# Tiny softmax sums, first value sums and three scales moved between engines in a two-level attention + two-FFN kernel

## The chip, the cores and the metric

The kernel runs on one core of one Trainium2 chip, in one launch. The metric is device time in microseconds (us), from three executions of each kernel. The engines are TensorE (PE; its weight loads are shown as PEld), VectorE (DVE), ScalarE (ACT), GpSimd (POOL) and SyncE (SP, which here issues nearly all DMAs). Each engine runs its own instructions in the order in which they were written down; they meet through semaphores.

## The reference

```python
# q, k, v: (4, 8, 576, 64) float32
q_d, k_d, v_d = means of four neighbouring rows               # 144 rows
out_up  = repeat(sm_attn(q_d, k_d, v_d), 4)                   # pooled attention
attn    = softmax(scale * q @ k.T where |i - j| < 4)          # local attention, 7 keys
a = a / (sum(a) + 1e-9)                                       # in both softmaxes
x = (out_up + attn @ v) as 2304 tokens x 512
h = x @ w_in;  g = where(h > 0, h, exp(min(h, 0)) - 1);  x = g @ w_out       # 512 -> 2048 -> 512
h = x @ w_in2; r = max(h, 0); g = s * r * r + b;         out = g @ w_out2
```

## The kernel before, in words

**Feed-forward part.** The 2304 tokens are nine blocks of 256. Each of the two FFNs (phases 0 and 1) works through 16 slices of 128 of the 2048 hidden columns for each block, so there are 144 pairs of block and slice in a phase. For each pair `ffn_h` issues 12 matmuls into a PSUM tile `h` and `ffn_x` 12 (phase 0) or 6 (phase 1, twice as wide) into `acc`. Every operand is split into a high and a low part of lower precision, hence three passes: `gh` and `gl` are the two parts of the activation, `w` holds both parts of a weight slice, which VectorE, ScalarE and GpSimd make from the loaded `raw` tile (L322 to L362).

**Attention part.** A unit is a pair of heads (`hp` 0 to 3) of one batch. Batch 0 runs first, before any FFN matmul can start: `tr` (transposes by TensorE, four-row sums by VectorE, L507), `gs` (pooled scores and their softmax, L542), `ls` and `softmax` (local scores, L625 and L647), `gpt_`/`lpt_` (transposes of the probabilities), `gpv`/`lpv` (times values, L604 and L705). The values summed in fours (`vd`) are needed by `gpv`. For batch 0 `vsum_pe` (L522) makes them with four matmuls by the identity per unit; for the other batches `vsum` (L533) makes them with two additions on GpSimd or VectorE. Batches 2 and 3 do the local attention without matmuls, in `direct` (L743). The second half of batch 0 and the batches 1 to 3 run between the FFN matmuls of phase 0.

**The sums.** Where ScalarE makes the exponentials, it also gives their sums (`sm`, an accumulator output); VectorE then adds 1e-9 and takes the reciprocal (L577, L685, L808).

**The order.** `Plan` (L55) takes every operation with an estimated cost and a due time (worked out from the constants at L29 to L32), plays them through and writes each engine's instructions down in the order it finds; it also picks between engines where an operation allows two. Where it sees TensorE idle, it puts filler matmuls on zeros (`wz`, L1131), as many as fill the planned gap. So every change of a cost or a constant reorders the whole program.

Of the kernel before, what the change touches and what calls it, by code (L numbers as in the profile page):

```python
# [6 lines left out]
F32 = mybir.dt.float32  # L7
# [21 lines left out]
T0, P0, LB, TR, R0, P1, P2 = 39.33, 5.045, 7, 29.37, 2.362, 2.546, 2.787  # L29
VO, N0, N1, WL, RL, A1, A2, A3, AE, XL = 13.82, -3.67, 51.83, 11.29, -7.8, 22.57, -17.87, 9.47, 64.11, 29.67  # L30
DE, DS, DT = 13.42, 98.08, 74.69
LASTP, NREST, VP = 2, 3, 2.0  # L32
# [22 lines left out]
class Plan:  # L55
# [172 lines left out]
def attn_moe_moe2(ctx, tc, q, k, v, w_in, w_out, w2_in, w2_out, s2, b2, mask, mask_d, out):  # L228
# [33 lines left out]
    ring = [p1.tile([QB, NQB, 2, D], F32, name=f"p{i}") for i in range(NLP)]  # L262
    nbufs["ring"] = NLP
# [110 lines left out]
    class Unit:  # L374
# [167 lines left out]
        def gs(self, heads, halves, due):  # L542
# [11 lines left out]
            nm, sm, s4, rs = (Buf(p2, t, [G, N2, 1]) for t in ("gnm", "gsm", "gs4", "grs"))  # L554
# [10 lines left out]
            op("dve", (0.1 + 0.15 * n) * len(heads) + 0.13 * (sc != 1.0), most, r=pss, w=[nmp], u=[nm], due=due)  # L565
# [14 lines left out]
            op("dve", 0.29, d2, r=[sm], w=[s4, rs], due=due)  # L580
# [4 lines left out]
        def gpt_(self, heads, halves, due):  # L585
# [14 lines left out]
            copy(pt, ps, 2 * n * m * G, r=[ps], w=[pt], due=due)  # L600
# [46 lines left out]
        def softmax(self, pss, half, due):  # L647
            F = 2 * NQB
            n = F * SW
            sc = Buf("ring", "p", None)  # L650
            sc.ring = ring
            part = lambda a: sc()[:, :, a, :SW]
            every = lambda: sc().rearrange("p m a w -> p (m a) w")[:, :, :SW]
            mx, sm, rs = (Buf(p2, t, [QB, F, 1]) for t in ("lmx", "lsm", "lrs"))

            by_act = self.b == 0 and self.hp % 2 < ACT_EXP
            for a, ps in enumerate(pss):
                h = slice(a, F, 2)
                if by_act:
# [28 lines left out]
            op("dve", 0.29 if by_act else 0.5 + n / 960, d2, r=[sc, sm], w=[sm, rs], due=due)  # L688
# [16 lines left out]
        def lpv(self, half, due):  # L705
# [10 lines left out]
            op("pe", 0.75, pe, r=[self.vwp[half], self.lpt[half]], w=[ps], u=self.both, due=due)  # L716
# [26 lines left out]
    def direct(b, t, due):  # L743
# [32 lines left out]
        sc = Buf(p2, "ds", [128, 4, 7])  # L776
# [8 lines left out]
        def scores(j):  # L785
# [5 lines left out]
                out=sc()[:, j:j + 2], in_=x(), axis=AX.X, op=ALU.add), r=[x], w=[sc], due=due)  # L791
# [11 lines left out]
        op("dve", 0.35, d1, r=[sc, c_sb2], w=[sc, mx], due=due)  # L803
        op("act", 0.2, lambda: nc.scalar.activation(out=sc(), in_=sc(), func=ACTF.Exp, scale=SCALE), r=[sc], w=[sc], due=due)

        def d2():
            nc.vector.tensor_reduce(out=sm()[:, :, 0], in_=sc(), axis=AX.X, op=ALU.add)
            nc.vector.tensor_scalar(out=sm(), in0=sm(), scalar1=1e-9, scalar2=None, op0=ALU.add)  # L808
            nc.vector.reciprocal(out=sm(), in_=sm())
            nc.vector.tensor_tensor(out=sc(), in0=sc(), in1=bc(sm), op=ALU.mult)  # L810

        op("dve", 0.75, d2, r=[sc], w=[sc, sm], due=due)

        def values(j):
# [3 lines left out]
               r=[vo, sc], w=[x], u=[rows_], due=due)  # L818
# [45 lines left out]
    def ffn_h(ph, j, f, n=N):  # L864
# [14 lines left out]
        us = 0.0075 + n / 2311  # L879
# [14 lines left out]
        if ph == 0:  # L894
            op("act", ta, lambda: nc.scalar.activation(out=e(), in_=ps(), func=ACTF.Relu, scale=-1.0),  # L895
# [19 lines left out]
    def ffn_x(ph, j, f, g):  # L915
# [5 lines left out]
        for a in range(2):  # L921
# [15 lines left out]
            op("pe", 0.70, pe, r=[w.out, gh, gl, acc], w=[acc], u=[w], due=due, ffn=True)  # L937
# [56 lines left out]
    def attention0():  # L994
# [12 lines left out]
        def Bs(u, d):  # L1007
            u.gs((0, 1), first, d), u.ls(0, d), u.vsum_pe(d + VP)
# [187 lines left out]
```

## Time and profile before

| | |
|---|---|
| median of 3 runs | 994.69 us (989.42 to 995.15) |
| the profiled execution | 995.36 us, of which the span is 993.6 us |
| busy share of the span | PE 97%, PEld 90%, DVE 64%, ACT 48%, POOL 41% |
| granted clock of TensorE, mean | 0.985 of full |
| first FFN matmul | 52.33 us after the span's start |

The busy time of TensorE counts fillers too, and counts a matmul at half clock in full. The 40 slices of the page show a clock of 0.8 and 0.5 in the first two slices and 0.9 or more in all others.

### The profile page before, as it was taken

To read this page: it belongs to the slowest core of one execution; us is meant where nothing else is said; L and a number is where in the kernel's file an instruction comes from. 1 tells how busy PE (TensorE), PEld (TensorE's weight loads), DVE (VectorE), ACT (ScalarE), POOL (GpSimd) and SP (SyncE) were. 2 spreads that over 40 slices of the span, in tenths; PEclk is the share of its full clock that TensorE was granted. 3 is DMA by queue.
4 is the path that set the end of the run, shared out by engine and by line. 5 is a ranking of instruction groups with operands and counts; after the bars stand their busy time and mean duration, and the time that the engine had idled before them with its cause. 6 is when DMAs were issued, how large, how long until landed. Compare 5 with 4: busy or idle time off the path is not lost.

```text
span 993.6 us, 21541 instructions
## 1 busy us (share of the span) xinstructions
PE 965.5 (97%) x8480; PEld 893.2 (90%) x8480; DVE 634.1 (64%) x1112; ACT 472.2 (48%) x1227; POOL 405.1 (41%) x358
## 2 busy tenths in 40 slices
PE   8999899998999999999999999999999999999998
PEld 6798888988989989999999999999999999999997
DVE  3478978888898989999637788433333343434332
ACT  4567566436444455444666675433333333333332
POOL 1245554688677787778465563100000000000000
PEclk8599999999999999999999999999999999999999
DMA  9556566435443353333335354001001010100000
GB/s 209 107 150 165 143 180 176 122 108 157 111 105 92 89 132 95 86 106 108 103 105 171 114 169 143 22 1 43 20 25 35 10 43 1 44 1 22 1 23 21
DMA packets 102469, 88.35 MB, mean 89 GB/s; under 512 B 48864, under 2 KB 91872, under 8 KB 102368
## 3 DMA queue, kind: packets, MB, share of 16 engines
q1 hardware_dynamic: 100576, 86.54, 31.4%
q8 instruction: 66, 1.08, 0.5%
q10 hardware_dynamic: 1792, 0.44, 0.2%
q14 instruction: 35, 0.29, 0.1%
HBM read 73.85 MB, written 13.11 MB: 88 GB/s over the span
## 4 chain that ended last, share of the span: by engine, by line
PE 48%; issue 3%; POOL 3%; DVE 3%; ACT 1%; SPq 0%; DMA 0%; POOLq 0%; DVEq 0%; ACTq 0%
PE h L875 24%; PE acc L934 20%; PE acc L931 4%; POOL gl L300 1%; POOL wu L300 1%; POOL w L300 1%; DVE raw L819 1%; DVE raw L351 1%; DVE r L899 0%; ACT raw L292 0%; DVE raw L353 0%; ACT r L895 0%; ACT w L292 0%; DVE wu L300 0%; ACT r L897 0%
## 5 line engine op out<-in xcount | busy, mean ns | idle before, releaser
L875 PE MATMUL h<-x,w 128*128 128x256 f32 x3264 | 430.6, 281 | 13.1 <-DVE r L899 10.8
L875 PEld LDWEIGHTS h<-x,w 128*128 128x128 f32 x3264 | 408.0, 188 | 30.7 <-DVE r L899 13.7
L931 PE MATMUL acc<-gh,w 128*128 128x256 f32 x1152 | 186.1, 283 | 0.0
L934 PE MATMUL acc<-w,gh 128*128 128x512 f32 x576 | 181.0, 395 | 0.0
L931 PEld LDWEIGHTS acc<-gh,w 128*128 128x128 f32 x1152 | 155.0, 188 | 2.5 <-issue 2.3
L905 DVE SCALAR_TENSOR_TENSOR r<-r,sb,h 128x256 f32<-128x256 f32 x144 | 68.8, 479 | 129.7 <-ACT r L904 128.6
L300 POOL TENSOR_TENSOR x<-xr,x 128x256 fp32r<-128x256 f32 (+2 forms) x43 | 43.1, 1021 | 264.0 <-DVE x L294 256.3
L300 POOL TENSOR_TENSOR gl<-r,gh 128x256 fp32r<-128x256 f32 x118 | 113.5, 967 | 59.3 <-ACT gh L292 52.5
L910 DVE SCALAR_TENSOR_TENSOR gl<-r,sb,gh 128x256 fp32r<-128x256 f32 x144 | 73.9, 513 | 99.2 <-ACT gh L908 99.2
L908 ACT ACTIVATE gh<-r,sb 128x256 fp32r<-128x256 f32 x144 | 73.4, 510 | 98.5 <-PE acc L934 89.4
L904 ACT ACTIVATE r<-h 128x256 f32<-128x256 f32 x144 | 55.1, 383 | 134.9 <-PE h L875 133.9
L931 PE MATMUL acc<-gl,w 128*128 128x256 f32 x576 | 114.4, 280 | 0.3 <-POOL gl L300 0.3
L934 PE MATMUL acc<-w,gl 128*128 128x512 f32 x288 | 114.0, 396 | 0.0
L934 PEld LDWEIGHTS acc<-w,gh 128*128 128x128 f32 x576 | 98.2, 188 | 14.1
L895 ACT ACTIVATE r<-h 128x256 f32<-128x256 f32 x144 | 54.7, 380 | 96.5 <-PE h L875 47.2
L300 POOL TENSOR_TENSOR w<-raw,w 128x512 fp32r<-128x512 f32 x47 | 64.2, 1379 | 78.7 <-ACT w L292 74.1
L899 DVE SCALAR_TENSOR_TENSOR r<-r,h 128x256 f32<-128x256 f32 x144 | 58.0, 412 | 49.4 <-ACT r L897 47.2
L931 PEld LDWEIGHTS acc<-gl,w 128*128 128x128 f32 x576 | 87.8, 188 | 0.9 <-POOL gl L300 0.7
L292 ACT ACTIVATE gh<-r 128x256 fp32r<-128x256 f32 x144 | 58.2, 413 | 52.6 <-DVE r L899 32.7
L934 PEld LDWEIGHTS acc<-w,gl 128*128 128x128 f32 x288 | 54.0, 188 | 13.0
L300 POOL TENSOR_TENSOR wu<-raw 128x896 f32<-128x896 f32 x29 | 61.5, 2135 | 9.3 <-DVE raw L819 9.3
L819 DVE TENSOR_REDUCE raw<-wu 128x128 f32<-128x896 f32 x36 | 63.5, 1783 | 2.1 <-POOL wu L300 2.0
(136 smaller groups left out, 1149.3 us busy)
## 6 DMA issues: line engine op xcount, KB each, us to landing
raw<-in_moe_w_in_dram SPq DMA_DIRECT2D x32, 512.0 KB
raw<-in_moe_w_out_dram SPq DMA_DIRECT2D x32, 512.0 KB
raw<-in_k_dram SPq DMA_DIRECT2D x17, 320.0 KB
raw<-in_v_dram SPq DMA_DIRECT2D x17, 320.0 KB
x2d<-ev SPq DMA_DIRECT2D x18, 256.0 KB
xr<-x2d SPq DMA_DIRECT2D x18, 256.0 KB
out_dram<-ev SPq DMA_DIRECT2D x16, 256.0 KB
vg<-in_v_dram SPq DMA_DIRECT2D x12, 288.0 KB
```

The lines of the kernel that those rows point to most:

```text
L292: a = (0.11 + n / 1200, lambda: nc.scalar.activation(out=out(), in_=src(), func=ACTF.Copy, scale=scale))
L300: f = lambda e: lambda: e.tensor_tensor(out=out(), in0=in0(), in1=in1(), op=alu)
L819: op("dve", 0.07 + 14 * D / 546, lambda: nc.vector.tensor_reduce(out=vo()[:, WD + j * D:WD + (j + 2) * D].rearrange("p (j d) -> p j d", j= ...
L875: nc.tensor.matmul(ps(), lhsT=w()[:, wpart, 0, c * 128:(c + 1) * 128], rhs=x()[:, xpart, c, :], start=first and i == 0, stop=last and i == ...
L895: op("act", ta, lambda: nc.scalar.activation(out=e(), in_=ps(), func=ACTF.Relu, scale=-1.0), r=[ps], w=[r1], u=[e], due=due)
L899: op("dve", td, lambda: nc.vector.scalar_tensor_tensor(out=e(), in0=e(), scalar=-1.0, in1=ps(), op0=ALU.add, op1=ALU.max), r=[r2, ps], w=[ ...
L904: op("act", ta, lambda: nc.scalar.activation(out=e(), in_=ps(), func=ACTF.Relu), r=[ps], w=[r1], u=[e], due=due)
L905: op("dve", td + 0.07, lambda: nc.vector.scalar_tensor_tensor(out=e(), in0=e(), scalar=sb2[:, 0:1], in1=ps(), op0=ALU.mult, op1=ALU.mult), ...
L908: op("act", ta + 0.1, lambda: nc.scalar.activation(out=gh(), in_=e(), func=ACTF.Identity, bias=sb2[:, 1:2]), r=[r2], w=[gh], u=[e], due=due)
L910: op("dve", td + 0.07, lambda: nc.vector.scalar_tensor_tensor(out=gl(), in0=e(), scalar=sb2[:, 1:2], in1=gh().bitcast(F32), op0=ALU.add, o ...
L931: nc.tensor.matmul(acc()[:, c * N:(c + 1) * N], lhsT=wo[:, cc * 128:(cc + 1) * 128], rhs=g(), start=(f == 0 and i == 0 and c == 0), stop=l ...
L934: nc.tensor.matmul(acc(), lhsT=g()[:, a * 128:(a + 1) * 128], rhs=wo, start=(f == 0 and i == 0), stop=last)
```

## The change

1. `vsum_pe` is gone; batch 0 uses `vsum` like the others, in place, with GpSimd or VectorE.
2. The tiles into which ScalarE writes sums are kept for the whole program, with a second column beside each sum that is filled with 1e-9 once; VectorE reduces the two columns (`TENSOR_REDUCE`) where it added a constant before (`TENSOR_SCALAR`). In the softmaxes that VectorE sums itself, 1e-9 stands in the column behind the scores and is summed with them.
3. The factor 4 of the pooled softmax moves into the eviction of the transposed probabilities (0.25 in `gpt_`); the factor on the row maxima moves from VectorE to ScalarE.
4. Costs of the planner, its due-time constants and the order that follows from them are changed.

```diff
-T0, P0, LB, TR, R0, P1, P2 = 39.33, 5.045, 7, 29.37, 2.362, 2.546, 2.787
+T0, P0, LB, TR, R0, P1, P2 = 39.86, 4.909, 5, 35.22, 2.265, 2.616, 2.881
...
-    GROUP = 9.0
+    GROUP = 12.52
...
+             "gsm": [p1.tile([G, 2, 2], F32, name=f"gsm{i}") for i in range(2)],
+             "lsm": [p1.tile([QB, 2 * NQB, 2], F32, name=f"lsm{i}") for i in range(2)],
+             "ds": [p1.tile([128, 4, 8], F32, name=f"ds{i}") for i in range(2)]}
...
-        def vsum_pe(self, due):
...
-                for r in range(4):
-                    nc.tensor.matmul(ps(), lhsT=ident[:G, :G], rhs=self.vg()[:, :, r * D:(r + 1) * D],
-                                     start=(r == 0), stop=(r == 3))
...
-               r=[self.vg], w=[self.vg, self.vd], due=due, lock=True)
+               r=[self.vg], w=[self.vg, self.vd], u=self.both + self.tdv if self.b == 0 else (), due=due, lock=True)
...
-                if sc != 1.0:
-                    nc.vector.tensor_scalar(out=nm(), in0=nm(), scalar1=sc, scalar2=None, op0=ALU.mult)
...
+                    if j == 0 and sc != 1.0:
+                        nc.scalar.activation(out=nm(), in_=nm(), func=ACTF.Copy, scale=sc)
...
-                nc.vector.tensor_scalar(out=s4(), in0=sm(), scalar1=1e-9, scalar2=4.0, op0=ALU.add, op1=ALU.mult)
+                nc.vector.tensor_reduce(out=s4()[:, :, 0], in_=sm()[:, :N2], axis=AX.X, op=ALU.add)
...
-            copy(pt, ps, 2 * n * m * G, r=[ps], w=[pt], due=due)
+            copy(pt, ps, 2 * n * m * G, scale=0.25, r=[ps], w=[pt], due=due)
...
-                if not by_act:
-                    nc.vector.tensor_reduce(out=sm()[:, :, 0], in_=every(), axis=AX.X, op=ALU.add)
-                nc.vector.tensor_scalar(out=rs(), in0=sm(), scalar1=1e-9, scalar2=None, op0=ALU.add)
+                x = sm() if by_act else sc().rearrange("p m a w -> p (m a) w")[:, :, :SW + 1]
+                nc.vector.tensor_reduce(out=rs()[:, :, 0], in_=x, axis=AX.X, op=ALU.add)
...
-            nc.vector.tensor_reduce(out=sm()[:, :, 0], in_=sc(), axis=AX.X, op=ALU.add)
-            nc.vector.tensor_scalar(out=sm(), in0=sm(), scalar1=1e-9, scalar2=None, op0=ALU.add)
+            nc.vector.tensor_reduce(out=sm()[:, :, 0], in_=ds(), axis=AX.X, op=ALU.add)
...
-            u.gs((0, 1), first, d), u.ls(0, d), u.vsum_pe(d + VP)
+            u.gs((0, 1), first, d), u.ls(0, d), u.vsum(d + VP)
...
+        for t in rings["gsm"] + rings["lsm"] + rings["ds"]:
+            nc.gpsimd.memset(t, 1e-9)
+        for t in rings["p"]:
+            nc.gpsimd.memset(t[:, :, :, SW:SW + 1], 1e-9)
```

How the order moves, at three places. First TensorE in the attention of batch 0, before the first FFN matmul. Here `w_287` and `w_302` are the loaded values of a unit, `w_150` its loaded queries and keys, `w_360` its transposed ones, `s` the pooled and `p` the local probabilities. The kernel before:

```order
L512 MATMUL at<-ident,w_150 128x96 x3
L527 MATMUL acc<-w_287,ident 72x256 x4
L595 MATMUL h<-ident,s 72x72 x4
L612 MATMUL h<-pt,w_209 64x72 x4
L550 MATMUL acc<-w_360 72x144 x2
L713 MATMUL h<-pt,w_224 64x32 x18
```

The same stretch in the changed kernel:

```order
L523 MATMUL at<-ident,w_293 128x96 x3
L598 MATMUL h<-ident,s 72x72 x4
L615 MATMUL h<-pt,w_224 64x72 x4
```

The sum by the identity (L527) no longer stands between the transposes and the products; there are four such rows of four matmuls in the kernel before and none in the changed one.

Second GpSimd at the start of the program, the kernel before (`lrs` and `grs` are the reciprocals of the sums):

```order
L1142 MEMSET p_87 96x384
masks.py:197 MEMSET ident 128x128
masks.py:199 ISA
masks.py:199 AFFINE_SELECT ident<-ident 128x128
L300 TENSOR_TENSOR p_85<-p_85,lrs 96x6x38
L300 TENSOR_TENSOR s<-s,grs 72x288 x2
```

And the changed kernel:

```order
L1149 MEMSET p_87 96x6
masks.py:197 MEMSET ident 128x128
masks.py:199 ISA
masks.py:199 AFFINE_SELECT ident<-ident 128x128
L536 TENSOR_TENSOR w_160<-w_160 72x4x128
L537 TENSOR_TENSOR w_224<-w_160 72x256
L311 TENSOR_TENSOR p_85<-p_85,lrs 96x6x38
L311 TENSOR_TENSOR s<-s,grs 72x288
L536 TENSOR_TENSOR w_242<-w_242 72x4x128
L537 TENSOR_TENSOR w_306<-w_242 72x256
```

The two additions of each unit (L536, L537) stand ahead of the normalizations in GpSimd's queue; nine small memsets more stand ahead of the identity.

Third VectorE in the softmaxes of the first unit, the kernel before:

```order
L685 TENSOR_SCALAR lrs<-lsm 96x6
L686 RECIPROCAL lrs<-lrs 96x6
L577 TENSOR_SCALAR gs_345<-gsm 72x2
L578 RECIPROCAL grs<-gs_345 72x2
```

And the changed kernel:

```order
L686 TENSOR_REDUCE lrs<-lsm_90 96x6
L687 RECIPROCAL lrs<-lrs 96x6
L580 TENSOR_REDUCE gs_362<-gsm_88 72x2
L581 RECIPROCAL grs<-gs_362 72x2
```

The constant is now read from the tile beside the sum, by a reduction.

Over the whole program VectorE has 949 rows where it had 1012, GpSimd 282 where it had 262, ScalarE 1004 where it had 968. The fillers, counted in TensorE's order, stand at other places, though there are 599 where there were 588: 187 before the first FFN matmul (153 before the change); 231 (376) from there to the 721st FFN matmul; 110 (27) from the 721st to the 865th, a stretch that holds the start of the third token block (its first matmul is the 769th); 71 (32) after that. SP issues the values of a unit (288 KB and 216 KB) ahead of the next unit's keys and queries, where it issued the keys and queries of all four units first.

## Rows read from the trace of the kernel before

**Rows 1.** The page: busy time, share and instructions of TensorE.
```profile
PE 965.5 (97%) x8480; PEld 893.2 (90%) x8480; DVE 634.1 (64%) x1112; ACT 472.2 (48%) x1227; POOL 405.1 (41%) x358
```

**Rows 2.** Busy time by stretch: length, PE, PEld, DVE, ACT, POOL, clock, DMA share, GB/s.
```profile
16.00:46.00 30.00, 30.00 (x298) 21.54 (x297) 12.39 (x38) 15.69 (x67) 7.43 (x11) 0.50 0.69 153
75.00:100.00 25.00, 23.60 (x418) 21.53 (x417) 20.46 (x41) 18.07 (x64) 14.27 (x14) 1.00 0.60 161
100.00:225.00 125.00, 117.25 (x1515) 108.84 (x1513) 106.32 (x202) 69.69 (x178) 76.99 (x68) 1.00 0.54 145
225.00:475.00 250.00, 241.17 (x2101) 232.81 (x2097) 228.82 (x358) 123.83 (x364) 192.38 (x155) 1.00 0.41 107
600.00:990.00 390.00, 389.57 (x2492) 350.79 (x2490) 154.66 (x311) 141.38 (x308) 25.43 (x26) 1.00 0.07 24
```

**Rows 3.** Timeline of TensorE: start, length, line, operands, count, idle before.
```profile
5.38 0.69 PE L512 MATMUL at<-ident,w 96*128 96x96 f32 x6
...
14.92 3.48 PE L527 MATMUL acc<-w,ident 72*72 72x256 f32 x8
18.33 0.76 PE L550 MATMUL acc<-w 64*72 64x144 f32 x4
...
39.47 3.62 PE L527 MATMUL acc<-w,ident 72*72 72x256 f32 x8
42.89 3.78 PE L1135 MATMUL at<-wz 128*128 128x128 bf16 x40
...
52.33 0.95 PE L875 MATMUL h<-x,w 128*128 128x256 f32 x6
...
62.68 1.74 PE L1135 MATMUL at<-wz 128*128 128x128 bf16 x28
```

**Rows 4.** Durations (ns, min/median/max) of the two additions on GpSimd, later batches.
```profile
L536 POOL TENSOR_TENSOR vg<-vg x10: 1270/1373/2273, 78.7 to 376.3; 72x512 f32<-72x512 f32 x10
L537 POOL TENSOR_TENSOR vd<-vg x10: 722/736/1568, 80.1 to 377.8; 72x256 f32<-72x256 f32 x10
```

**Rows 5.** Groups of VectorE by form: busy us, mean ns; idle before.
```profile
L577 DVE TENSOR_SCALAR gs<-gsm 72x2 f32<-72x2 f32 x32 | 18.2, 569 | 1.5 <-ACT s L571 1.2
L685 DVE TENSOR_SCALAR lrs<-lsm 96x6 f32<-96x6 f32 x16 | 5.7, 354 | 1.9 <-ACT p L667 1.6
L563 DVE TENSOR_SCALAR gnm<-gnm 72x2 f32<-72x2 f32 x16 | 5.0, 313 | 0.5
L808 DVE TENSOR_SCALAR dsm<-dsm 128x4 f32<-128x4 f32 x18 | 4.6, 255 | 0.6
L807 DVE TENSOR_REDUCE dsm<-ds 128x4 f32<-128x28 f32 x18 | 3.2, 176 | 0.3 <-ACT ds L804 0.3
```

**Rows 6.** Timeline of GpSimd and VectorE around 404 us.
```profile
403.53 1.69 POOL L300 TENSOR_TENSOR wu<-raw,ds 128x896 f32<-128x896 f32 x1 [2.61 <-issue]
403.68 1.56 DVE L577 TENSOR_SCALAR gs<-gsm 72x2 f32<-72x2 f32 x1
```

**Rows 7.** Waits of TensorE over the span: total us, times, longest.
```profile
PE h L875 <- DVE r L899: 10.8, 15, 2.3
```

**Rows 8.** Timeline of GpSimd at the start: memsets and the identity.
```profile
0.34 0.11 POOL L1179 MEMSET const-uint8-127<- 128x1 uint8 x1
0.73 1.12 POOL L1142 MEMSET p<- 96x384 f32 x3 [0.29 <-POOLq L1179]
...
2.07 0.29 POOL masks.py:199 TENSOR_SCALAR_AFFINE_SELECT ident<-ident 128x128 f32<-128x128 f32 x1
```

**Rows 9.** Timeline of ScalarE: its smallest activation.
```profile
4.18 0.20 ACT L1017 ACTIVATE warm<-wz 128x1 bf16<-128x1 bf16 x1
```

**Rows 10.** Timeline of TensorE at the third token block.
```profile
227.10 3.30 PE L875 MATMUL h<-x,w 128*128 128x256 f32 x24
```

**Rows 11.** Two stretches of 4 us, columns as in Rows 2.
```profile
12.00:16.00 4.00, 2.98 (x19) 2.07 (x20) 2.12 (x7) 2.45 (x8) 1.19 (x2) 0.88 0.98 195
96.00:100.00 4.00, 2.98 (x54) 2.63 (x50) 1.12 (x4) 2.34 (x6) 2.56 (x2) 1.00 0.25 100
```

More of the change, by code (lines that the diff above doesn't have):

```diff
@@ L61 @@
     SLACK = 0.0
-    GROUP = 9.0
-    SWITCH = 0.024
-    HOLD = 0.089
-    WAIT = 1.512
+    GROUP = 12.52
+    SWITCH = 0
+    HOLD = 0.057
+    WAIT = 1.597
     STORE = 2.5
@@ L261, in attn_moe_moe2, with kept @@
     msk = p1.tile([QB, 2, NQB, SW], BF16, name="msk")
-    ring = [p1.tile([QB, NQB, 2, D], F32, name=f"p{i}") for i in range(NLP)]
-    nbufs["ring"] = NLP
+    rings = {"p": [p1.tile([QB, NQB, 2, D], F32, name=f"p{i}") for i in range(NLP)],
+             "gsm": [p1.tile([G, 2, 2], F32, name=f"gsm{i}") for i in range(2)],
+             "lsm": [p1.tile([QB, 2 * NQB, 2], F32, name=f"lsm{i}") for i in range(2)],
+             "ds": [p1.tile([128, 4, 8], F32, name=f"ds{i}") for i in range(2)]}
+    for tag, tiles in rings.items():
+        nbufs[tag] = len(tiles)
+    def kept(tag):
+        b = Buf(tag, tag, None)
+        b.ring = rings[tag]
+        return b
     mskd = p1.tile([128, 2, 28], BF16, name="mskd")
@@ L553, in gs @@
             op("pe", 0.25 * N2 / len(heads) + 0.1, pe, r=[self.d], w=pss, u=self.tdv, due=due)
-            nm, sm, s4, rs = (Buf(p2, t, [G, N2, 1]) for t in ("gnm", "gsm", "gs4", "grs"))
+            nm, s4, rs = (Buf(p2, t, [G, N2, 1]) for t in ("gnm", "gs4", "grs"))
+            sm = kept("gsm")
             e = Buf(p2, "s", [G, N2, 2 * G])
@@ L561, in most @@
                     nc.vector.tensor_reduce(out=nm()[:, j * n:(j + 1) * n, 0], in_=ps(), axis=AX.X, op=ALU.max, negate=True)
[L562 to L565 removed]
+            op("dve", (0.1 + 0.15 * n) * len(heads), most, r=pss, w=[nmp], u=[nm], due=due)
             for j, ps in enumerate(pss):
                 def ac(j=j, ps=ps):
+                    if j == 0 and sc != 1.0:
+                        nc.scalar.activation(out=nm(), in_=nm(), func=ACTF.Copy, scale=sc)
                     for i in range(n):
@@ L649, in softmax @@
             n = F * SW
-            sc = Buf("ring", "p", None)
-            sc.ring = ring
+            sc = kept("p")
             part = lambda a: sc()[:, :, a, :SW]
             every = lambda: sc().rearrange("p m a w -> p (m a) w")[:, :, :SW]
-            mx, sm, rs = (Buf(p2, t, [QB, F, 1]) for t in ("lmx", "lsm", "lrs"))
+            mx, rs = (Buf(p2, t, [QB, F, 1]) for t in ("lmx", "lrs"))
             by_act = self.b == 0 and self.hp % 2 < ACT_EXP
+            sm = kept("lsm") if by_act else None
             for a, ps in enumerate(pss):
@@ L714, in pe @@
                                          rhs=pt[o:o + SW, i * SB:(i + 1) * SB], start=True, stop=True)
-            op("pe", 0.75, pe, r=[self.vwp[half], self.lpt[half]], w=[ps], u=self.both, due=due)
+            op("pe", 1.24, pe, r=[self.vwp[half], self.lpt[half]], w=[ps], u=self.both, due=due)
             x = Buf(p2, "xs", [128, G, 4])
@@ L775, in direct @@
         load(vo, 327680, lambda: window(v, vo), due - 6, u=[rows_])
-        sc = Buf(p2, "ds", [128, 4, 7])
+        ds = kept("ds")
+        sc = Buf(None, "sc", None)
+        sc.view = lambda: ds()[:, :, :7]
         mx, sm = (Buf(p2, x, [128, 4, 1]) for x in ("dmx", "dsm"))
@@ L877, in mm @@
             return pe
-        us = 0.0075 + n / 2311
+        us = 0.0085 + n / 2311
         w_hi, w_lo = w.part
@@ L935, in pe @@
                                          start=(f == 0 and i == 0), stop=last)
-            op("pe", 0.70, pe, r=[w.out, gh, gl, acc], w=[acc], u=[w], due=due, ffn=True)
+            op("pe", 0.712, pe, r=[w.out, gh, gl, acc], w=[acc], u=[w], due=due, ffn=True)
             if f == FC - 1:
@@ L1140, in attn_moe_moe2 @@
         nc.vector.memset(wz, 0.0)
-        for t in ring:
+        for t in rings["p"]:
             nc.gpsimd.memset(t, 0.0)
+        for t in rings["gsm"] + rings["lsm"] + rings["ds"]:
+            nc.gpsimd.memset(t, 1e-9)
+        for t in rings["p"]:
+            nc.gpsimd.memset(t[:, :, :, SW:SW + 1], 1e-9)
         make_identity(nc, ident)
```

37 lines of the change are left out of this document (18 added, 19 removed).

## The prediction

> **What bounds the kernel now.** I read the page first, then the busy time by stretch, then TensorE's timeline at the start, then the groups of VectorE, and last the waits. TensorE is busy in 965.5 of 993.6 us [rows 1], so the time is the length of its instruction stream plus 28.1 us of idle. From 600 us on there is nothing to gain: 389.57 of 390 us are busy, and these are FFN matmuls alone [rows 2]; the change leaves them as they are. What can move lies before 600 us, in two places. One is the start. From 16 to 46 us TensorE is busy without a gap, at a granted clock of 0.50, that is 1.2 instead of 2.4 GHz [rows 2], and the first FFN matmul stands at 52.33 us [rows 3]. In this stretch TensorE itself is the bound: VectorE works 12.39 of 30 us, ScalarE 15.69, GpSimd 7.43. The other place is the stretch from 75 to 475 us. There TensorE's idle is 1.40 + 7.75 + 8.83 = 18.0 us, and VectorE is the fullest of the engines that feed it: 228.82 of 250 us in the last part [rows 2].
>
> **The change part by part.** The sum is made against the profiled execution, 995.36 us, which lies 0.1% above the median of 994.69.
>
> *The value sums leave TensorE.* One of them takes from 14.92 to 18.33 us, 3.41 us from its first matmul to the next instruction, and the last one from 39.47 to 42.89, 3.42 us [rows 3]. There are four: 4 x 3.42 = 13.7 us of a stream that has no gap here. I take the whole, **-13.7 us**. At the high clock the same columns would take about half, so an end of -6.8 us stands for a start that isn't throttled.
>
> *Fillers.* The changed order has 34 more before the first FFN matmul (187 against 153). At the low clock 40 fillers take 3.78 us [rows 3], 94.5 ns each: **+3.2 us**. After it there are 23 fewer (412 against 435), and at the high clock 28 take 1.74 us [rows 3], 62 ns each: **-1.4 us**. Their places matter more than their number: 145 fewer up to the 721st FFN matmul (-9.0 us), 83 more around the start of the third block (+5.1), 39 more behind it (+2.4).
>
> *The sums arrive on GpSimd.* The two additions have medians of 1.37 and 0.74 us [rows 4], 2.1 us a unit, 8.4 us for four. GpSimd is idle for three quarters of the start, so most of it is covered. But GpSimd runs in order, and the normalizations `p` and `s` stand behind the additions, which in turn wait for their values to land; TensorE's next transposes wait for `p` and `s`. If one of the four sums shows, that is 2.1 us; if none, 0; if all, 8.4. I take **+2 us**, since GpSimd has only 7.43 us of other work in 30 us.
>
> *The loads change places.* 504 KB of values now stand ahead of the keys and queries of the third unit. The DMA engines move 195 GB/s there [rows 11], so these come about 2.6 us later. At worst the third unit's transposes wait all of it, at best they would have waited for something else until then; between 0 and 2.6 us I take **+1 us**, the lower half, since the queue in front of them is the same length otherwise.
>
> *The memsets at the start.* Nine more stand ahead of the identity, which is ready at 2.36 us [rows 8]; TensorE first uses it at 5.38 us [rows 3]. The nearest small memset takes 0.11 us, the wide ones 0.4 [rows 8], so the identity moves to 3.4 us, or to 6.0 at worst. Zero, or 0.6 us if the cover is gone.
>
> *VectorE's small operations.* An operation on two elements a lane, `gs`, takes 569 ns on average and 18.2 us in all [rows 5], because it is held up: one began at 403.68 and lasted 1.56 us, until 5.24, while an addition on GpSimd ran from 403.53 to 405.22 [rows 6]. A reduction of 28 elements to 4 takes 176 ns, evenly [rows 5]. With 176 ns for each reduction, `gs` gives back 32 x (569 - 176) = 12.6 us, `gnm` 5.0 (it goes to ScalarE), `dsm` 4.6 (it falls away), `lrs` 5.7 - 8 x 0.176 = 4.3 (eight fall away, eight become reductions): 26.5 us of VectorE's time. The Trainium skill speaks against this edit (VectorE: DVE Perf Modes, Rules for kernel authors): a reduction runs at the lowest rate and is the slowest operation of VectorE, so restructure. By that rule nothing of the 12.6 us would come back; the rows above decide for the reduction at these sizes. On the path I count the 26.5 us as **0**: TensorE's idle in this stretch is small, and a held operation may only hand its hold-up to the next one. At most it is TensorE's own waiting for `r` of VectorE, 10.8 us [rows 7]; at least nothing, since less work on VectorE costs nobody time. The 16 scalings on ScalarE take 0.20 us each [rows 9], 3.2 us in all, while four evictions of the value sums go; ScalarE is half idle, and in the chain of one softmax the scaling only changes its engine. Zero. GpSimd takes over some splits from VectorE; it works 192.38 of 250 us from 225 to 475 us [rows 2], so its spare time covers them. The 0.25 rides on an eviction that is there anyway. Zero each.
>
> Sum: -13.7 + 3.2 - 1.4 + 2 + 1 = -8.9 us, and 995.36 - 8.9 = **986.4 us**.
>
> **The rivals.**
>
> *VectorE was the bound in the middle.* For it: VectorE is 92% busy from 225 to 475 us, and TensorE's largest wait in the list is the one for its `r`, 10.8 us [rows 2, 7]. Against it: TensorE itself is 96% busy there. If that goes as well, the time is 986.4 - 10.8 = 975.6 us. The Trainium skill has a rule that weakens this rival (SBUF: State Buffer, SBUF: two separate sides): VectorE and GpSimd share one port pair, which one instruction holds to its end. The trace agrees, with 1.56 us at 403.68 [rows 6], and an operation with two inputs that follows would be held in the same way.
>
> *The third block doesn't come earlier, and the kernel is slower.* The first FFN matmul of the third block stands at 227.10 us [rows 10]. Its input is what the attention of batch 1 wrote to memory, a chain through all engines in which VectorE is 106.32 of 125 us busy [rows 2]. If that chain isn't shortened, everything won before is waited away there, and the changed order itself stalls at this place with 110 fillers where there were 27. What is left is the 39 later fillers, +2.4 us: 997.8 us. It decides as soon as the third block starts no earlier than 227 us. Against it: the chain starts from the same attention of batch 0, which ends earlier, and VectorE has less to do. Partly true, it would end between 987 and 995.
>
> *The clock falls a second time.* Before the fall at about 15.5 us TensorE was busy 2.98 of 4 us, and the low clock then lasted until about 46 us [rows 2, 11]. The changed order has 145 fewer fillers between the first FFN matmul and the third block. If TensorE really waits there, 30 us at half clock cost 15 us: 986.4 + 15 = 1001.4 us. Against it: from 96 to 100 us it was also busy only 2.98 of 4 us and the clock stayed at 1.00 [rows 11].
>
> *GpSimd doesn't keep up at the start.* All four sums show, 6.4 us more: 992.8 us. It is in the forecast's range.
>
> **How the numbers follow.** Chances: the forecast 0.50, VectorE as the bound 0.25, the third block partly or wholly unmoved 0.19, the clock 0.06. The forecast's own range is 980 to 993: down to 980.1 where nothing new is waited for (3.0 us) and a third of the 10.8 us comes back (3.6), up to 993 where all four sums show. From 975 to 997 the range takes in VectorE's case and the third block's but for its far end. A difference of 1%, 10 us, is about what a measurement of this kernel can tell from no change; it lies at 984.7 us, inside the forecast's range. So faster by over 1% has VectorE's 0.25 and a third of the forecast, 0.41 together; slower by over 1% needs the clock and more, 0.05; within 1% the rest, 0.54.
>
> **What would show it.** Right: no matmuls by the identity into `acc`, the first FFN matmul at 43 to 48 us, the reductions `gs` at 0.15 to 0.2 us each, the third block at 215 to 222 us, and 390 us that are the same from there on. Wrong at the sums: TensorE idle behind `p` or `s` of GpSimd before 45 us. Wrong at VectorE: the same idle of TensorE although VectorE's busy time falls by 25 us, or idle that falls below 10 us. Wrong at the third block: its first matmul at 227 us. The clock: a second stretch at 0.5.

## The result and the profile after

The changed kernel takes 983.21 us (median of 20 runs, 980.57 to 987.69), the kernel before 994.4 us on the same chips (20 runs, 984.55 to 998.75). The ratio is 0.9911, 95% interval [0.9887, 0.9934]: 8.9 us less, which is the forecast's sum to the tenth. (The medians differ by 11.2: the runs of the kernel before lie in three groups, about 985, 989 and 994 us and up, and the ratio weighs them all.) That the sum came out so is luck: the experiments show errors of both signs that cancelled. The profiled span is 981.8 us (993.6 before).

The page of the changed kernel, busy time of each engine, to be held against [rows 1]:

```profile
PE 961.0 (98%) x8459; PEld 897.8 (91%) x8459; DVE 614.9 (63%) x1055; ACT 475.3 (48%) x1242; POOL 409.6 (42%) x387
```

TensorE has 961.0 of 981.8 us busy, so 20.8 us idle instead of 28.1. That is only 4.5 us less busy time, although 13.7 us of value sums are gone: something else on TensorE has become longer.

Busy time by stretch, columns as in [rows 2]:

```profile
12.00:16.00 4.00, 3.47 (x68) 2.86 (x68) 2.80 (x11) 2.70 (x12) 2.98 (x4) 1.00 1.20 214
16.00:46.00 30.00, 29.54 (x508) 26.72 (x506) 20.11 (x44) 19.76 (x81) 17.98 (x20) 0.94 0.88 216
75.00:100.00 25.00, 24.16 (x300) 22.22 (x297) 23.06 (x36) 17.93 (x47) 16.06 (x16) 1.00 0.54 163
100.00:225.00 125.00, 118.86 (x1454) 111.08 (x1455) 107.06 (x194) 71.81 (x194) 75.90 (x75) 0.99 0.57 157
225.00:475.00 250.00, 246.57 (x2112) 240.64 (x2111) 206.63 (x314) 120.37 (x344) 182.33 (x150) 1.00 0.37 100
```

The largest difference is in the second row: from 16 to 46 us the clock is 0.94 instead of 0.50, and TensorE gets through 508 instructions instead of 298. In the whole profile the clock falls three times before the last microseconds, at about 31, 62 and 212 us, for 3.4 us each. From 75 to 475 us TensorE is idle for 0.84 + 6.14 + 3.43 = 10.4 us instead of 18.0.

TensorE's timeline, columns as in [rows 3]: the load that the values now stand ahead of, the first FFN matmul, and the start of the third block (cf. [rows 10]):

```profile
12.47 0.79 PE L523 MATMUL at<-ident,w 96*128 96x96 f32 x6 [0.76 <-DMA w<-in_k_dram]
...
32.69 3.14 PE L1138 MATMUL acc<-wz 128*128 128x128 bf16 x36
35.64 0.95 PE L878 MATMUL h<-x,w 128*128 128x256 f32 x6
...
202.62 1.90 PE L1138 MATMUL acc<-wz 128*128 128x128 bf16 x31
204.33 1.22 PE L878 MATMUL h<-x,w 128*128 128x256 f32 x8
```

The first FFN matmul stands 16.7 us earlier (52.33 before), the third block 22.8 us (227.10 before). The kernel ends only 11.8 us earlier. The rest is lost again.

GpSimd at the start, columns as in [rows 8]: the identity, the first unit's two additions, and the normalization behind them:

```profile
2.44 0.29 POOL masks.py:199 TENSOR_SCALAR_AFFINE_SELECT ident<-ident 128x128 f32<-128x128 f32 x1
9.41 1.27 POOL L536 TENSOR_TENSOR w<-w 72x512 f32<-72x512 f32 x1 [6.68 <-DMA w<-in_v_dram]
10.76 0.73 POOL L537 TENSOR_TENSOR w<-w 72x256 f32<-72x256 f32 x1
11.85 0.56 POOL L311 TENSOR_TENSOR p<-p,lrs 96x228 f32<-96x228 f32 x1 [0.36 <-DVE gs L580]
```

The additions wait for the values to land, but the normalization behind them then waits for VectorE (0.36 us), not for them.

VectorE's groups, columns as in [rows 5]: the three reductions, and two operations with two inputs that follow or stand near them:

```profile
L311 DVE TENSOR_TENSOR w<-raw,w 128x512 fp32r<-128x512 f32 x17 | 21.9, 1288 | 1.1 <-ACT w L303 1.1
L814 DVE TENSOR_TENSOR ds<-ds,dsm 128x28 f32<-128x28 f32 x18 | 7.6, 421 | 0.6
L580 DVE TENSOR_REDUCE gs<-gsm 72x2 f32<-72x4 f32 x32 | 4.6, 144 | 2.4 <-ACT s L572 2.3
L810 DVE TENSOR_REDUCE dsm<-ds 128x4 f32<-128x32 f32 x18 | 3.2, 180 | 2.0 <-ACT ds L807 2.0
L686 DVE TENSOR_REDUCE lrs<-lsm 96x6 f32<-96x12 f32 x8 | 1.2, 154 | 0.9 <-ACT p L669 0.9
```

The reductions take 144 to 180 ns, as forecast. Other operations became longer: `ds` now takes 421 ns (271 before), `w` by L311 1288 (882 before). VectorE's busy time fell by 19.2 us, not by 26.5. Whether a hold-up passed to them or the new order did it, a_ts tells below.

The waits of TensorE and GpSimd, columns as in [rows 7]:

```profile
POOL w L536 <- DMA w<-in_v_dram: 7.8, 3, 6.7
PE h L878 <- DVE r L902: 5.3, 6, 1.7
PE at L699 <- POOL p L311: 1.5, 3, 0.8
PE at L598 <- POOL s L311: 1.4, 4, 0.8
```

TensorE's wait for `r` halved (10.8 before). For GpSimd's `p` and `s` it waits 2.9 us in all.

**What got longer.** Twelve `h` matmuls of the second FFN and the matmul behind them, the kernel before and the changed kernel (timeline of TensorE):

```profile
800.41 1.56 PE L875 MATMUL h<-x,w 128*128 128x256 f32 x12
801.81 0.63 PE L934 MATMUL acc<-w,gh 128*128 128x512 f32 x2
```

```profile
803.08 1.60 PE L878 MATMUL h<-x,w 128*128 128x256 f32 x12
804.52 0.63 PE L937 MATMUL acc<-w,gh 128*128 128x512 f32 x2
```

From the first of the twelve to the next instruction it was 1.40 us and is now 1.44. Over the whole second FFN, one `h` matmul follows the other after 117.0 ns on average before, 120.5 ns after; from ScalarE's first `gh` of that phase to its last it took 398.9 us (586.3 to 985.2) and now takes 403.8 (569.6 to 973.4). These matmuls are the same in both kernels, at a clock of 1.00. What differs is where their operands lie in SBUF: the six kept tiles of the sums, less the tiles that they replace, push `x`, `r`, `gh` and `gl` from 160 to 224 bytes past a multiple of 256 (the addresses that the built programs give).

### The profile page after: what moved, and what is told of

Same layout as the page of the kernel before. It is cut to its first block, busy times and chain, and to the rows that moved or that the text cites. A ratio compares the mean times of both kernels' runs of the same rounds, so it can differ in the third digit from the quotient of the medians.

```text
span 981.8 us, 21481 instructions
## 1 busy us (share of the span) xinstructions
PE 961.0 (98%) x8459; PEld 897.8 (91%) x8459; DVE 614.9 (63%) x1055; ACT 475.3 (48%) x1242; POOL 409.6 (42%) x387
## 4 chain that ended last, share of the span: by engine, by line
PE 75%; DVE 8%; issue 5%; POOL 5%; ACT 2%; DMA 2%; SPq 0%; ACTq 0%; POOLq 0%; DVEq 0%
PE h L878 35%; PE acc L937 21%; PE acc L934 13%; POOL gl L311 2%; DVE raw L362 2%; POOL w L311 1%; DVE raw L364 1%; DMA w<-in_k_dram 1%; PE acc L1138 1%; PE at L714 1%; PE at L523 1%; PE at L615 1%; DVE r L902 1%; DVE raw L357 1%; DVE raw L822 1%
## 5 line engine op out<-in xcount | busy, mean ns | idle before, releaser
L878 PE MATMUL h<-x,w 128*128 128x256 f32 x3264 | 441.9, 285 | 6.1 <-DVE r L902 5.3
L878 PEld LDWEIGHTS h<-x,w 128*128 128x128 f32 x3264 | 419.2, 189 | 22.3 <-DVE r L902 7.7
L934 PE MATMUL acc<-gh,w 128*128 128x256 f32 x1152 | 188.3, 285 | 0.0
L934 PEld LDWEIGHTS acc<-gh,w 128*128 128x128 f32 x1152 | 157.5, 189 | 1.6 <-issue 1.2
L311 POOL TENSOR_TENSOR gl<-r,gh 128x256 fp32r<-128x256 f32 x131 | 119.8, 919 | 89.0 <-ACT gh L303 76.2
L311 POOL TENSOR_TENSOR x<-xr,x 128x256 fp32r<-128x256 f32 (+2 forms) x47 | 43.4, 944 | 267.2 <-DVE x L305 257.9
L913 DVE SCALAR_TENSOR_TENSOR gl<-r,sb,gh 128x256 fp32r<-128x256 f32 x144 | 77.7, 540 | 103.9 <-ACT gh L911 103.9
L311 POOL TENSOR_TENSOR w<-raw,w 128x512 fp32r<-128x512 f32 x47 | 65.9, 1415 | 58.3 <-ACT w L303 52.9
L900 ACT ACTIVATE r<-r 128x256 f32<-128x256 f32 x144 | 60.1, 417 | 4.1
```

The source lines that it names most:

```text
L311: f = lambda e: lambda: e.tensor_tensor(out=out(), in0=in0(), in1=in1(), op=alu)
L878: nc.tensor.matmul(ps(), lhsT=w()[:, wpart, 0, c * 128:(c + 1) * 128], rhs=x()[:, xpart, c, :], start=first and i == 0, stop=last and i == ...
L900: op("act", ta, lambda: nc.scalar.activation(out=e(), in_=e(), func=ACTF.Exp, scale=-1.0), r=[r1], w=[r2], u=[e], due=due)
L913: op("dve", td + 0.07, lambda: nc.vector.scalar_tensor_tensor(out=gl(), in0=e(), scalar=sb2[:, 1:2], in1=gh().bitcast(F32), op0=ALU.add, o ...
L934: nc.tensor.matmul(acc()[:, c * N:(c + 1) * N], lhsT=wo[:, cc * 128:(cc + 1) * 128], rhs=g(), start=(f == 0 and i == 0 and c == 0), stop=l ...
```

## The experiments

Theory: the change is worth more than 8.9 us, and gives part of it back because the FFN's tiles lie at a slower place. Rivals: the changed order or the instructions themselves slow the matmuls; or the parts of the change are worth what the forecast gave each. All ratios are to runs of the kernel before on the same chip; a time "over the changed kernel" is a difference of medians, to its 983.21 us.

**Place of the tiles, in the changed kernel** (64, 32 and 96 bytes that nothing uses, in front of the large tiles):

```diff
+    pad = p1.tile([128, 16], F32, name="pad")     # 8 for a_pad32, 24 for a_pad96
```

a_pad64:

> The changed kernel with one unused tile of 64 bytes a lane ahead of the large tiles, so that every tile behind it stands at the same address modulo 128 bytes as in the kernel before (x, gh, gl at 32; in the changed kernel they stand at 96). The instructions and their order are the same. Theory (address): the matmuls of the changed kernel follow each other 120 ns apart instead of 117 because of where their moving operand lies; with this tile the distance goes back to 117 ns, the second FFN from its first to its last gh takes 399 us instead of 404, phase 0 loses another 5 to 9 us, and the time is 969 to 973 us. Rival (the chip or the run): the distance stays at 120 ns and the time at 983 us.

Measured 977.47 us (976.87 to 984.27, 6 runs), ratio 0.9871 [0.9828, 0.9915]; 117.6 ns from `h` to `h`, 401.1 us for the second FFN. The pace comes back to within a per cent of the kernel before, and the time falls by 5.7 us, less than the 10 to 14 that I expected.

a_pad32:

> The same with 32 bytes: x, gh, gl, nat stand at 0 (x, gh, gl) and 64 (nat) modulo 128. Theory (address): if what counts is that a row of the moving operand starts on a boundary, the distance falls below 117 ns, to 110 to 114, and the time to 945 to 965 us; if it is only a matter of 32 against 96, it lies at 117 to 120 and the time at 969 to 983. Rival (the run): 120 ns, 983 us.

Measured 980.2 us (978.34 to 984.73, 6 runs), ratio 0.9893 [0.9848, 0.9937]; 119.4 ns: pace and time lie between the changed kernel and a_pad64, and no boundary shows.

a_pad96:

> The same with 96 bytes: x, gh, gl stand at 64 modulo 128, nat at 0. Theory (address): as with 32 bytes if 64-byte boundaries are what counts (110 to 114 ns, 945 to 965 us), else between 117 and 120 ns. Rival (the run): 120 ns, 983 us.

Measured 965.64 us (965.39 to 967.09, 6 runs), ratio 0.9735 [0.9699, 0.977]; 115.4 ns, between the two paces that I had expected. The same twelve matmuls take 1.38 us:

```profile
800.85 1.55 PE L879 MATMUL h<-x,w 128*128 128x256 f32 x12
802.23 0.62 PE L938 MATMUL acc<-w,gh 128*128 128x512 f32 x2
```

No instruction differs between these kernels, and 17.6 us lie between the changed kernel and the one with 96 bytes more. 10.1 of them lie in the second FFN (403.8 against 393.7 us). It is the best version of all, by the medians 28.8 us under the kernel before.

**The same place in the kernel before** (b_pad64: `x` and `gh` at 224 modulo 256, as in the changed kernel; the same line with 16):

> The kernel before with the unused tile of 64 bytes: x, gh, gl move from 32 to 96 modulo 128, nat from 96 to 32. Theory (address): the distance goes from 117 to 120 ns, the second FFN from 399 to 404 us, and the kernel gets 8 to 14 us slower, 1002 to 1008 us. Rival (the run, or the other edits of the change): 117 ns, 994 us.

Measured 1000.21 us (991.89 to 1006.38, 12 runs), ratio 1.0067 [1.0032, 1.0102]; 120.5 ns and 403.9 us for the second FFN, the changed kernel's own numbers. So the slower matmuls come from the place, and neither from the order nor from the edits: 0.67%, 6.7 us, just under the 8 to 14 that I expected.

Its profile shows a second thing. Its stretch from 16 to 46 us and its first value sum:

```profile
16.00:46.00 30.00, 29.43 (x468) 24.52 (x467) 19.73 (x46) 18.86 (x78) 12.12 (x15) 0.89 0.93 219
```

```profile
14.47 1.89 PE L528 MATMUL acc<-w,ident 72*72 72x256 f32 x8
16.30 0.47 PE L551 MATMUL acc<-w 64*72 64x144 f32 x4
```

In this execution the clock stayed at 1.00 over the sums, and one took 1.83 us from its start to the next instruction (3.41 in [rows 3]); the clock fell only at about 38 us, for 6.8 us, and once more at 89 us, for 3.4. ScalarE's first `gh` stood at 47.9 us, against 57.8 in the profile of the kernel before: 9.9 us by the clock, with the same instructions in the same order.

**Part 1 alone** (b_vsum: the value sums by GpSimd or VectorE in the kernel before, replanned by its own constants):

```diff
-            u.gs((0, 1), first, d), u.ls(0, d), u.vsum_pe(d + VP)
+            u.gs((0, 1), first, d), u.ls(0, d), u.vsum(d + VP)
-               r=[self.vg], w=[self.vg, self.vd], due=due, lock=True)
+               r=[self.vg], w=[self.vg, self.vd], u=self.both + self.tdv if self.b == 0 else (), due=due, lock=True)
```

> Part 1 alone: the kernel before with the value sums of batch 0 on GpSimd or VectorE; constants, costs, softmax sums and the places of the tiles as before. The planner orders anew and puts 708 fillers in (588 before), 201 of them ahead of the first FFN matmul. Theory (the sums and the low clock they prolonged): the first FFN matmul comes at 38 to 44 us instead of 52, since TensorE gives up 6.8 us at the high clock or 13.7 at the low one, and matmuls stay 117 ns apart; 120 more fillers give 7 us back; 984 to 990 us. Rival (the retuned constants make the gain): 992 to 996 us. Rival (GpSimd doesn't keep up): idle of TensorE behind p or s at the start, over 995 us.

Measured 987.92 us (982.77 to 993.6, 12 runs), ratio 0.9976 [0.9941, 1.0011]; clock from 16 to 46 us in its profile 0.89:

```profile
16.00:46.00 30.00, 28.14 (x492) 25.75 (x492) 19.24 (x46) 18.23 (x76) 17.39 (x20) 0.89 0.79 190
```

The first FFN matmul stands at 39.34 us, as expected. No run has a mean clock under 0.988, so in this order, which also has 48 more fillers ahead of the first FFN matmul, the long fall is gone; whether the sums or the fillers do it isn't separated. Shorter falls remain (6.8 us at about 25 and 353 us). GpSimd's work from 16 to 46 us rises from 7.43 to 17.39 us [rows 2]. At a clock of 0.996 or more, though, part 1 gains nothing: 985.8 us (median of five runs) against 984.8 for the kernel before.

**Part 1 undone** (a_vsum_pe: the sums back on TensorE in the changed kernel, same constants):

```diff
+        def vsum_pe(self, due): ...
-            u.gs((0, 1), first, d), u.ls(0, d), u.vsum(d + VP)
+            u.gs((0, 1), first, d), u.ls(0, d), u.vsum_pe(d + VP)
```

> Part 1 undone: the changed kernel with the sums by the identity on TensorE again (591 fillers, 106 of them ahead of the first FFN matmul); all else, the places of the tiles too, as changed. Theory: 6.8 us more where the clock at the start stays high, 988 to 991 us, and 994 to 999 where it falls there. Rival (the constants and the small sums made the gain): 982 to 986 us.

Measured 985.67 us (982.75 to 997.05, 12 runs), ratio 0.9959 [0.992, 0.9998]: 2.5 us over the changed kernel, which is the rival's time and not the theory's. The first FFN matmul stands at 37.64 instead of 35.64 us. The clock from 16 to 46 us is 0.94 here too, and 11 of the 12 runs have a mean clock of 0.995 or more (one has 0.982, and 997.05 us). So in the changed order the sums on TensorE mostly don't bring the long fall back. They take 1.8 to 1.9 us each, and 81 fillers fewer stand at the start (106 against 187): about 7.4 us at 1.85 less 5.0 at the 62 ns of [rows 3].

**The small sums undone** (a_ts: a constant added by `TENSOR_SCALAR` again, in the changed kernel's order and tiles):

```diff
-                nc.vector.tensor_reduce(out=s4()[:, :, 0], in_=sm()[:, :N2], axis=AX.X, op=ALU.add)
+                nc.vector.tensor_scalar(out=s4(), in0=sm()[:, :N2, 0:1], scalar1=1e-9, scalar2=None, op0=ALU.add)
...
-            nc.vector.tensor_reduce(out=sm()[:, :, 0], in_=ds(), axis=AX.X, op=ALU.add)
+            nc.vector.tensor_reduce(out=sm()[:, :, 0], in_=sc(), axis=AX.X, op=ALU.add)
+            nc.vector.tensor_scalar(out=sm(), in0=sm(), scalar1=1e-9, scalar2=None, op0=ALU.add)
```

> Part 2 undone on VectorE alone: the changed kernel in which 1e-9 is added as a constant again (TENSOR_SCALAR on the first column; in the local softmaxes one instruction more), with the same costs given to the planner, so that the order on every engine is the same. Theory of the prediction: VectorE's busy time rises by 15 to 26 us, gs to 0.4 to 0.6 us each, and the time by less than 3 us, 982 to 986 us. Rival (VectorE bounds the middle): TensorE's idle from 75 to 475 us rises by 8 us or more, 990 us or more.

Measured 991.81 us (988.48 to 997.36, 12 runs), ratio 1.002 [0.9984, 1.0057]: 8.6 us over the changed kernel. Its groups of VectorE (and the spread of one, here and in the changed kernel, columns as in [rows 4]), its waits of TensorE and the line of its page:

```profile
L580 DVE TENSOR_SCALAR gs<-gsm 72x2 f32<-72x2 f32 x32 | 13.2, 414 | 2.6 <-ACT s L572 2.5
L812 DVE TENSOR_SCALAR dsm<-dsm 128x4 f32<-128x4 f32 x18 | 6.1, 340 | 0.6
L816 DVE TENSOR_TENSOR ds<-ds,dsm 128x28 f32<-128x28 f32 x18 | 7.1, 393 | 0.6
L311 DVE TENSOR_TENSOR w<-raw,w 128x512 fp32r<-128x512 f32 x17 | 15.4, 906 | 1.1 <-ACT w L303 1.1
```

```profile
L580 DVE TENSOR_SCALAR gs<-gsm x32: 132/165/1542, 12.8 to 390.0; 72x2 f32<-72x2 f32 x32
```

```profile
L580 DVE TENSOR_REDUCE gs<-gsm x32: 129/144/155, 11.7 to 387.1; 72x2 f32<-72x4 f32 x32
```

```profile
PE h L880 <- DVE r L904: 7.3, 11, 1.7
PE at L700 <- POOL p L311: 3.3, 7, 0.8
PE at L598 <- POOL s L311: 2.7, 4, 1.7
```

```profile
PE 962.0 (97%) x8459; PEld 897.0 (91%) x8459; DVE 630.5 (64%) x1081; ACT 474.7 (48%) x1242; POOL 414.8 (42%) x387
```

VectorE is busy 15.6 us longer than in the changed kernel, and TensorE, with as many instructions, is idle 986.7 - 962.0 = 24.7 us instead of 20.8. Of the 4.9 us between the two profiled spans, 3.9 are such idle; the waits for VectorE's `r` and for `p` and `s`, which GpSimd scales by VectorE's reciprocals, are longer by 2.0, 1.8 and 1.3 us. So the small sums are on the path: for a third of their 15.6 us by the profiles, for a little over half by the medians. The theory's 982 to 986 us failed; the rival's time came, but not its mechanism, since idle from 75 to 475 us rises by 2.4 us and not by 8.

Only VectorE's instructions differ between the two kernels. For `gs` the quickest addition is as quick as the quickest reduction (132 and 129 ns), but one is held up to 1542 ns, and no reduction takes more than 155. The hold-up did pass on in part: `w` takes 906 ns here and 1288 in the changed kernel, 6.5 us in all. `ds` is slow here too, so its rise belongs to the changed order.

**The constants undone** (a_const: the due times and planner constants of the kernel before in the changed kernel):

```diff
-T0, P0, LB, TR, R0, P1, P2 = 39.86, 4.909, 5, 35.22, 2.265, 2.616, 2.881
+T0, P0, LB, TR, R0, P1, P2 = 39.33, 5.045, 7, 29.37, 2.362, 2.546, 2.787
...
-    GROUP = 12.52
+    GROUP = 9.0
```

> Part 4 undone: the changed kernel with the due-time constants and the planner's GROUP, SWITCH, HOLD and WAIT of the kernel before (the costs of single operations stay changed): 674 fillers (599), 225 ahead of the first FFN matmul, 518 up to the 721st (418). Theory (the order is worth its fillers): 75 fillers more are 4.7 us, so 986 to 990 us. Rival (the retuning makes most of the gain): 992 us or more.

Measured 993.45 us (990.55 to 996.87, 12 runs), ratio 1.003 [0.9996, 1.0064]: 10.2 us over the changed kernel, the rival's time. The clock from 16 to 46 us is 0.83 in its profile and no run has a mean over 0.993, so some of this is the clock: its three runs at 0.993 (median 991.0) lie 7.3 us over the changed kernel's three at 0.994 (983.7). The parts overlap: 2.5, 8.6 and 10.2 us add up to more than the whole change.

**Which place it is.** First the kernel before with 32 bytes (b_pad32, the line of the pads with 8) and the changed one with 224 (a_pad224, with 56):

> The kernel before with a tile of 32 bytes that nothing uses, so that x, r, gh and gl start at 64 modulo 128 bytes as in a_pad96 and not at 32 as in the kernel before; no instruction changes. If the place of the operands sets the pace of the FFN matmuls (theory): 115 to 115.5 ns from h matmul to h matmul (117.0 in the kernel before), second FFN about 394 us long (398.9), time 980 to 987 us; against a_pad96 (965.6) the change itself is then worth 15 to 20 us at equal places, more than the 8.9 us seen. If a_pad96 owes its gain to its own order of work meeting the shift (rival): cadence 117, time 990 to 998 us.

Measured 995.94 us (991.44 to 997.06, 12 runs), ratio 1.0038 [1.0005, 1.007]; 117.9 ns. The theory's number (115 to 115.5 ns, 980 to 987 us) failed.

> The changed kernel with a pad of 224 bytes in place of the 96 of a_pad96: all later tiles 128 bytes further, so x, gh at 64 and nat at 0 modulo 128 again, but another place modulo 256. If the place modulo 128 is what counts (theory): as a_pad96, cadence of h matmuls 115.4 ns and 964 to 968 us. If it is a place modulo 256 or more, or a single lucky collision-free place (rival): another cadence, 117 to 120.5 ns, and 975 to 984 us.

Measured 977.26 us (974.19 to 982.18, 6 runs), ratio 0.9857 [0.9797, 0.9917]; 117.9 ns. So the place modulo 128, by which I had reckoned, is not what counts. But the two kernels have the same pace, 1.42 and 1.41 us for the twelve:

```profile
800.36 1.57 PE L876 MATMUL h<-x,w 128*128 128x256 f32 x12
801.78 0.63 PE L935 MATMUL acc<-w,gh 128*128 128x512 f32 x2
```

```profile
800.49 1.57 PE L879 MATMUL h<-x,w 128*128 128x256 f32 x12
801.90 0.63 PE L938 MATMUL acc<-w,gh 128*128 128x512 f32 x2
```

In both, `x` and `gh` lie at 192 modulo 256. They also give the change at a second equal place: 0.9857 against 1.0038, 18 us, where the pair at 224 gives 0.9911 against 1.0067, 15.5 us. Both figures hold the clock's long fall as well: 11 of 12 runs of b_pad32 and 7 of 12 of b_pad64 have a mean clock of 0.985 or less, and none of the other two kernels has.

Then `x` and `gh` apart. a_padx holds `gh`, `gl` and `pt` back by a second pad, a_padg moves them alone:

```diff
+    pad3 = p3.tile([128, 24], F32, name="pad3")   # a_padx, with pad = p1.tile([128, 24], ...)
+    pad3 = p3.tile([128, 8], F32, name="pad3")    # a_padg, alone
```

> The changed kernel with x, r and raw at 64 modulo 128 bytes as in a_pad96, but gh, gl and pt held at 96 as in the changed kernel (a second pad in their pool). If each matmul goes by the place of its own operand (theory): h matmuls (which read x) at 115.4 ns, the second FFN's output matmuls (which read gh and gl) as in the changed kernel at about 234.8 ns for 512 columns, time halfway, 973 to 976 us. If the place of gh alone or that of x alone decides for all matmuls (rivals): 964 to 968 with both cadences fast, or 980 to 986 with both slow.

Measured 976.42 us (975.37 to 980.48, 6 runs), ratio 0.9852 [0.98, 0.9904]; `h` to `h` 117.7 ns, `gh` to `gh` matmuls of 512 columns 231.4 ns, `gh` to `gl` 234.9. (Modulo 256 `gh` lies at 96 here and at 224 in the changed kernel, so it is held at the changed kernel's place modulo 128 only.)

> The mirror of a_padx: gh, gl and pt at 64 modulo 128 bytes as in a_pad96, x, r, raw and nat left where the changed kernel has them (96, nat 32). If each matmul goes by the place of its own operand (theory): h matmuls stay at 120.4 ns, output matmuls of the second FFN at about 227 ns as in a_pad96 (234.8 in the changed kernel), time 973 to 976 us. If x decides for all: both slow and 980 to 986 us; if gh decides for all: both fast and 964 to 968 us.

Measured 976.47 us (976.02 to 986.42, 6 runs), ratio 0.9863 [0.9806, 0.9921]; `h` to `h` 119.3 ns, 231.8 and 227.1. Both times lie between the ends, just over the theory's 973 to 976 us, but not for its reason: with `x` at its best place and `gh` elsewhere, the `h` matmuls run at 117.7 ns and not at 115.4. The pace of a matmul is not set by the place of its own operand alone. What else takes part stays open; a pad moves every tile behind it, not only these two.

## Why the prediction was right, and where it was not

The time was right, 986.4 us forecast and 995.36 x 0.9911 = 986.5 by the ratio. Its parts were not:

- **The value sums, -13.7 us at the low clock: wrong in kind.** I took the low clock as a property of the start and priced four sums at it. It is an event, which the same program has in some executions and not in others, and both part 1 alone and the changed order with the sums on TensorE mostly do without it. What in them keeps it away is not shown. Runs of the kernel before with a mean clock of 0.996 or more take 984.8 us (median of 12), and 43 of its 69 runs beside the experiments have 0.985 or less, and 993.8 us and up. No run of the changed kernel is under 0.994. That the long fall doesn't happen is worth about 9.4 us (994.2, the median of the 69, less 984.8). The sums themselves, at the high clock, are worth 2.5 (a_vsum_pe), less than the end of 6.8 that I gave for a start that isn't throttled, since sums on TensorE partly take the place of fillers.
- **The fillers, +3.2 and -1.4 us: the first priced at the wrong clock.** At the 62 ns of the high clock 34 fillers are 2.1 us.
- **GpSimd, +2 us: too much.** TensorE waits 2.9 us for `p` and `s` over the span, and not at all before 45 us; in the kernel before it was 3.7 for `p` and 0.8 for `s`.
- **The loads, +1 us: about right.** TensorE waits 0.76 us for keys at 12.47. **The memsets, 0: right.** The identity is ready at 2.73 us instead of 2.36, and first used at 4.98.
- **VectorE's small operations, 0 on the path: the step that failed on the gain's side.** "TensorE's idle in this stretch is small" was read as "nothing to win", but a_ts gives 8.6 us, and 8.8 at a clock of 0.996 or more (991.6, median of three that spread from 988.5 to 992.1, against 982.8). The rival with VectorE as the bound priced it at 10.8 us and was nearer, though the wait for `r` fell to 5.3 us and not to nothing. VectorE's gain was read rightly (`gs`, `gnm`, `dsm` and `lrs` gave back 27.7 us for 26.5); what it does on the path was not. The Trainium skill's rule that a reduction is the slowest operation (VectorE: DVE Perf Modes, Rules for kernel authors) would have kept the old form; at two to four elements the reduction took 144 ns, the addition of a constant 414 to 569 on average, because it was held up at times.
- **"390 us that are the same from there on": failed.** The second FFN takes 4.9 us more. I looked at which instructions there are and in what order, and not at where their tiles lie. The diff showed it: six new kept tiles ahead of the large ones.
- **The places.** First FFN matmul at 35.64 instead of 43 to 48 us, third block at 204.33 instead of 215 to 222. In b_pad64's profile, without the long fall, the order of the kernel before has them at 40.40 and 218.54, so 11.9 of the 16.7 us and 8.6 of the 22.8 are the clock's. With the fall the first would have been about in its range, the second still ahead of it. The rival of an unmoved third block is out. That of a second fall came true in small, with the three falls of 3.4 us.
- **The range.** Its lower end is 979.8 by its own terms (986.4 - 3.0 - 3.6), not 980.1; nothing hangs on it.

By runs at equal clock (0.995 or more): the kernel before 984.8, with the tiles where the changed kernel has them 991.9 (two runs of b_pad64): +7.1. From there to the changed kernel, 982.8: -9.1, which is what its edits and its order are worth at equal place and clock. So at equal clock the whole change is worth 2.0 us. With -9.4 for the clock that is -11.4 us; the medians differ by 11.2. So -8.9 was forecast from the sums at a low clock, and came from a clock that mostly doesn't fall, from small operations and from the order, less what the tiles' new place took. That these meet at the forecast's number is luck.

Not settled: how the 9.1 us divide, since a_ts, a_const and a_vsum_pe overlap; what in the change keeps the long fall away; and why one place is faster than another.

## What to carry to other kernels

When a change adds or resizes a tile that is kept, compare the pace of the long matmul runs before and after, over some twelve of them; if it moved, try pads of 32 bytes before judging the change. A stretch at half clock is an event with its own price: ask for the time of a run without it, and don't put it down to the work that happens to stand in it. A held-up operation of two elements can be on the path even if the bound engine's idle is small; undoing it alone, in the same order, tells. A total that meets the forecast proves none of its terms.

## What the hardware showed that I had not expected

The pace of the same matmuls (128 x 128 weights, 256 columns, clock 1.00) goes by where the tiles lie. Mean time from `h` to `h` in the second FFN, and the length of that phase from ScalarE's first `gh` to its last:

| `x` and `gh`, bytes modulo 256 | kernels | ns | us |
|---|---|---|---|
| 64 | a_pad96 | 115.4 | 393.7 |
| 160 | before, b_vsum | 117.0 | 398.9, 398.9 |
| 32 | a_pad64 | 117.6 | 401.1 |
| 192 | b_pad32, a_pad224 | 117.9 | 400.3, 400.8 |
| 0 | a_pad32 | 119.4 | 402.0 |
| 224 | after, b_pad64, a_ts, a_vsum_pe, a_const | 120.5 | 403.8, 403.9, 403.9, 403.8, 405.7 |
| `x` 64, `gh` 96 | a_padx | 117.7 | 400.7 |
| `x` 224, `gh` 64 | a_padg | 119.3 | 400.0 |

Kernels with the same place modulo 256 agree in pace to the tenth, whatever the order of work; 64 and 192, the same modulo 128, differ by 2.5 ns. 96 and 128 were not tried for both. The tiles of the weights never moved; other tiles behind the pads did.

The clock's long fall is not fixed for a kernel: the same order of work had 0.50 from 16 to 46 us in one profile, 0.89 in that of b_pad64, and again 0.50 in that of b_pad32. In the stretch from 12 to 16 us ahead of the long fall TensorE was busy 2.98 us in both executions that fell ([rows 11] and b_pad32), and 3.35 us in b_pad64, which did not fall there (its row from 16 to 46 us stands above):

```profile
12.00:16.00 4.00, 2.98 (x27) 2.16 (x25) 2.39 (x8) 2.77 (x11) 1.19 (x2) 1.00 1.07 190
16.00:46.00 30.00, 30.00 (x298) 21.56 (x297) 12.39 (x38) 15.93 (x68) 7.48 (x11) 0.50 0.69 153
```

These two rows are b_pad32's, columns as in [rows 2]; from 96 to 100 us the kernel before was busy as little and kept its clock [rows 11], so what sets off the fall stays open.
